# Attention with a threshold, then a mixer: the last key tile stacked, six score buffers, a new order

## The chip, the cores and the metric

The kernel runs on one core of one Trainium2 chip. The metric is the device time in microseconds. The kernel before took 622.38 us (median of 3 runs, 621.68 to 625.62). A core has engines that run on their own: TensorE (PE, with its weight loads listed as PEld) multiplies matrices, VectorE (DVE) and ScalarE (ACT) work on tiles in the two on-chip memories SBUF and PSUM, GpSimd (POOL) works on tiles in SBUF and issues DMAs, SyncE (SP) issues DMAs.

## The reference

The input is q, k and v of 8 batches x 8 heads x 576 positions x 64, a number tau, and the weights of a mixer. The attention keeps only the scores within tau of the row's maximum; a low-rank product over the positions and a two-layer channel mixer follow.

```python
scores = scale * np.matmul(q, k.transpose(0, 1, 3, 2))           # scale = 1/8
thresh = np.max(scores, axis=-1, keepdims=True) - tau
scores = np.where(scores >= thresh, scores, -1000000000.0)
scores = scores - np.max(scores, axis=-1, keepdims=True)
attn = np.exp(scores)
attn = attn / (np.sum(attn, axis=-1, keepdims=True) + 1e-09)
x = np.matmul(attn, v)                  # then heads side by side: (8, 576, 512)
...
h = x.transpose(0, 2, 1) @ U @ V        # U: 576 x 32, V: 32 x 576
u = x + h.transpose(0, 2, 1)
out = u + np.maximum(u @ w_ch1, 0.0) @ w_ch2                     # 512 -> 2048 -> 512
```

## The kernel before

The kernel is written as tasks, each with an engine, a rough cost, what it depends on, and a function that issues its instructions. A scheduler inside the kernel (class `Order`) puts the tasks of each engine into one fixed order when the program is built. Among the tasks that can start, it takes the one with the lowest rank: the moment at which it is ready plus an offset `OFF` by kind of task and by phase (first batch, middle, last batch); the mixer's tasks have a `when`, a number of score steps from which they are due. Where TensorE would stand idle in the scheduler's reckoning, it puts in a filler matmul.

```python
def rank(c):
    s, t = c
    if t.when is not None:
        due = t.when <= steps + (1.0 if t.kind == kind else 0.0)
        return (t.when - 1000.0 if due else t.when + 1000000.0, s)
    return (t.ready + t.off, s)
...
while at[PE] + 0.45 < s and last[n] <= at[PE]:
    self.filler(n)
```

A pair is two heads of one batch; there are 32, four in a batch. Of a pair's 576 queries, four tiles of 128 rows and one of 64 are made; the 64-row tiles of two pairs are joined. So two pairs have nine score steps, 144 in all. A step computes the scores of two heads into PSUM (`scores`, on TensorE), and then, for each head:

```python
# weigh (VectorE): out of PSUM, times -scale, with the row's minimum
nc.vector.tensor_scalar(out=s_sb..., in0=pair_bank[x][:, :, 0:HC], scalar1=-scale, ...,
                        op0=ALU.mult, op1=ALU.min, accum_out=m[:, x:x + 1])
t = add(VEC, 0.69, weigh, [S_, got("w", tiles[0] + x - NS)])     # NS = 4 buffers s_sb
...
# exponential (ScalarE), threshold (ScalarE), then select (VectorE)
nc.scalar.activation(out=e_sb, in_=s_sb, func=ACT.Exp, bias=m[:, x:x + 1], scale=-1.0)
...
nc.vector.scalar_tensor_tensor(out=w_sb[:, 0:S], in0=s_sb, scalar=thr_[:, x:x + 1], in1=e_sb,
                               op0=ALU.is_le, op1=ALU.mult, accum_out=pr.den[:, i, x:x + 1])
```

The weights w_sb (128 queries x 576 keys, padded with zeros to 640) are transposed to keys x queries, by a DMA (`turn_w`) or, for some tiles, on TensorE (`turn_pe`, and `copy_w` on ScalarE). V is split into a high and a low half in bf16:

```python
def high(_):                                      # ScalarE
    nc.scalar.copy(out=pr.vh[:, :, :, 0, :], in_=pr.vraw.rearrange("p j t d -> p t j d"))
def low(_):                                       # GpSimd
    nc.gpsimd.tensor_tensor(out=pr.vh[:, :, :, 1, :],
                            in0=pr.vraw.rearrange("p j t d -> p t j d"),
                            in1=pr.vh[:, :, :, 0, :], op=ALU.subtract)
```

The product multiplies five key tiles (NT = 5, the last with 64 real keys and 64 zeros) with both halves. In the first four pairs (`soft`) the halves are two matmuls of 64 columns into the same place; in the 28 others they stand side by side as one of 128 columns, and their sum is made later (`low_part` on ScalarE, `join` on VectorE, `norm` on GpSimd; in the soft pairs one `make` on VectorE).

```python
for kt in range(NT):
    ...
    first, last_ = kt == 0, kt == NT - 1
    if not soft:
        nc.tensor.matmul(av[:, 2 * a + j, :], w, pr.vh[:, kt, j, :, :], start=first, stop=last_)
        continue
    for h in range(2):
        nc.tensor.matmul(av[:, 2 * a + j, :], w, pr.vh[:, kt, j, h, :],
                         start=first and h == 0, stop=last_ and h == 1)
```

After a pair: `narrow`, `low_rank`, `spread`, `sum_u`, `turn_u` make u and its transpose. After a batch the mixer: 16 groups `up` of four 512-column matmuls, with `relu` on ScalarE, and 4 or 5 tiles of `down` in four quarters of four 512-column matmuls each, with `finish` on VectorE and `send` as a DMA. Every second batch also has `rest`, the up-product of the joined 64-row tiles.

```python
t = add(PE, 0.862, up, uT + weights1 + ..., banks=1, kind="p1", when=due + 35.75 * ft / 16)
...
when = due + 134.5 if i == 4 and b < B - 1 else due + 46.5 + 13.25 * (i + g / 4) / 4
```

Of the kernel before, what the change touches and what calls it, by code (L numbers as in the profile page):

```python
# [8 lines left out]
P = 128  # L9
FP32 = mybir.dt.float32  # L10
BF16 = mybir.dt.bfloat16
# [20 lines left out]
DUE = (30, 48, 66, 87, 163, 120, 127, 156)  # L32
# [32 lines left out]
class Order:  # L65
# [10 lines left out]
    SWITCH = {"quadrants": 0.145, None: 0.095}  # L76
# [4 lines left out]
        "copy_main": (37, 30, -1), "copy_rest": (-1, -8, -1), "copy_tt": (-26, -59, -3),  # L81
        "copy_u": (-22, -16, -2), "copy_u4": (0, 21.25, 0), "copy_w": (39.75, -8, -1),
        "down": (0, 0, 0), "exponential": (21, 43, -29.25), "finish": (-1, 13, -1),
        "first": (-300, 0, 0), "high": (3, -26, -32), "inverse": (-19, 8.75, 8.5),
        "join": (-22, -3.25, 2.5), "load": (16, 20, 2), "low": (0, 0, 0),
        "low_part": (-22, -19.5, -40), "low_rank": (-20, -39, -3), "make": (8.25, -2, -2),
        "narrow": (-24, 15, -5), "narrow_u": (-21, 20.25, -1), "narrow_u4": (1, 9, 1),
        "norm": (-24, -1, -4), "product": (-21, 20, 8), "relu": (-2, -45, -2), "rest": (0, 0, 0),
        "scores": (-26, -69.5, -9), "select": (4.75, 49.25, 0.75), "send": (2, 2, 2),
        "spread": (-23, -7.25, -3), "spread4": (-1, 21, -1), "spread_v": (1, 5, 5),  # L90
        "sum_u": (-25, -11, 0), "sum_u4": (1, -4, 1), "sums": (-22, -1, -1),
        "threshold": (-27, -6, -29.5), "turn4": (-1, -1, -1), "turn_main": (-2, -37.75, -4),
        "turn_pe": (-25, 19.75, -1), "turn_rest": (-3, -38, -5), "turn_u": (-50, -6, -3),
        "turn_w": (-20, 0, 0), "up": (0, 0, 0), "values": (20, 20, 20), "weigh": (-23, -3, -8),
        "weights": (-4, 5, 5),
# [100 lines left out]
def kernel(  # L196
# [33 lines left out]
    idle = wpool.tile([P, 512], BF16, name="idle")  # L230
    nc.vector.memset(idle, 0.0)
# [13 lines left out]
    for t_ in w_ring:  # L245
        nc.vector.memset(t_[:, :, S:640], 0.0)
# [5 lines left out]
    for t_ in vraw_ring:  # L252
        nc.vector.memset(t_[HB:P, :, 4, :], 0.0)
# [16 lines left out]
    NS = 4  # L270
# [20 lines left out]
    def fill(n):  # L291
        nc.tensor.matmul(bank[n], idle[:, 0:P], idle, start=True, stop=True)  # L292
# [24 lines left out]
    def load_tasks(p, pr):  # L317
# [28 lines left out]
        for part, to, of in ((lo, slice(0, 5), slice(0, 5)), (hi, slice(0, 4), slice(5, 9))):  # L346
            def values(_, part=part, to=to, of=of):
                nc.sync.dma_start(pr.vraw[part, :, to, :], vv[:, :, of, :])

            loads["v"].append(add(SP, 0.7, values, freed, dma=0.55))  # L350
# [24 lines left out]
    def prepare_tasks(p):  # L375
# [37 lines left out]
        def low(_):  # L413
            nc.gpsimd.tensor_tensor(out=pr.vh[:, :, :, 1, :],  # L414
                                    in0=pr.vraw.rearrange("p j t d -> p t j d"),
                                    in1=pr.vh[:, :, :, 0, :], op=ALU.subtract)
# [3 lines left out]
        done["vlo", p] = add(POOL, 1.5, low, [t])  # L420
# [6 lines left out]
    def score_tasks(p, i):  # L427
# [51 lines left out]
        for x in range(2):  # L479
# [17 lines left out]
            both = not (p < EARLY and 1 <= i < 4)  # L497

# [14 lines left out]
            if i < 4 and (x == 1 and p < EARLY and i >= 1 or p == NPAIR - 1 and i == 3):  # L513
                t = done["wT", tiles[0]] = add(PE, 0.28, turn_pe, [sel] + free, banks=1,
                                               kind="wT")

                def copy_w(_, x=x, t=t):
                    nc.scalar.copy(
                        out=pr.wT[:, x, :, i * P:(i + 1) * P],
                        in_=bank[t.got[0]][:, 0:320].bitcast(BF16).rearrange(  # L520
                            "p (k r) -> p k r", k=NT))

                t = add(SCA, 0.68, copy_w, [t], frees=[t])
            elif both and not x:
                t = None
                first_sel = sel
            elif both:
                t = done["wT", tiles[0]] = done["wT", tiles[0] - 1] = add(
                    SP, 1.4, turn_w, [first_sel, sel] + free, dma=2.2)
            else:  # L530
                t = done["wT", tiles[0]] = add(SP, 1.28, turn_w, [sel] + free, dma=1.1)
            if t:
                done.setdefault(("wTs", p, i // 2), []).append(t)
                if i == 4:
                    done.setdefault(("wTs", p + 1, 2), []).append(t)
# [11 lines left out]
    def value_tasks(p):  # L547
# [16 lines left out]
        for g, tiles_ in enumerate(((0, 1), (2, 3), (4,))):  # L564
            n = len(tiles_)

            def product(t, tiles_=tiles_):

                av = bank[t.got[0]].rearrange("p (a m) -> p a m", m=D if soft else P)
                for a, i in enumerate(tiles_):  # L570
                    for j in range(2):
                        for kt in range(NT):
# [6 lines left out]
                            first, last_ = kt == 0, kt == NT - 1  # L579
                            if not soft:  # L580
                                nc.tensor.matmul(av[:, 2 * a + j, :], w, pr.vh[:, kt, j, :, :],  # L581
                                                 start=first, stop=last_)
                                continue
                            for h in range(2):
                                nc.tensor.matmul(av[:, 2 * a + j, :], w, pr.vh[:, kt, j, h, :],
                                                 start=first and h == 0, stop=last_ and h == 1)

            av = done["AV", p, g] = add(
                PE, (0.64 if soft else 0.56) * n, product,
# [229 lines left out]
    def weight_loads():  # L819
# [6 lines left out]
        sv = wpool.tile([R, S], FP32, name="sv")  # L826
# [88 lines left out]
```

## Time and profile before

| | busy, us | share of the 618.1 us span |
|---|---|---|
| TensorE matmuls (PE) | 607.7 | 98% |
| VectorE (DVE) | 521.3 | 84% |
| ScalarE (ACT) | 480.1 | 78% |
| GpSimd (POOL) | 290.2 | 47% |

The largest groups: 288 `select` on VectorE, 844 ns each in the mean; 288 `exponential` on ScalarE, 770 ns; 288 `weigh` on VectorE, 752 ns; the scores on TensorE; the mixer's `down` and `up`. Busy time is the union of an engine's instructions, and a matmul's record overlaps the next one's, so the mean of one is longer than the time from one to the next. In the lines shown later, `L461` is `weigh`, `L488` `select`, `L448` the scores, `L581` and `L585` the products with 128 and with 64 columns, `L749` `up`, `L782` `down`, `L414` `low`, `L292` the filler.

### The profile page before, as it was taken

The numbers are of one execution on the slowest core, as the hardware profiler recorded it, in microseconds if no ns is written. First come the engines' busy times: TensorE is split into PE (matmuls) and PEld (weight loads), VectorE is DVE, ScalarE is ACT, GpSimd is POOL, SyncE is SP. The second block draws the span as 40 slices with busy tenths as digits, with TensorE's granted clock in tenths as the row PEclk, the third lists the DMA queues.
The fourth block names the chain that finished last, engine by engine and source line by source line (L and its number), as shares of the span: only waits on it lengthen the run. The fifth ranks groups of instructions, "written<-read, shape, count | busy, mean of one in ns | idle before, by whom it ended". The sixth has DMA issues, their size and how long they took to land.

```text
span 618.1 us, 16905 instructions
## 1 busy us (share of the span) xinstructions
PE 607.7 (98%) x6363; PEld 351.8 (57%) x6363; DVE 521.3 (84%) x1406; ACT 480.1 (78%) x983; POOL 290.2 (47%) x396
## 2 busy tenths in 40 slices
PE   8989999999999999999999999999999999999997
PEld 4555655665666555555565655555466655555553
DVE  5999998799988999799997999899998889797101
ACT  5688899988899678986798877996779956884540
POOL 8976566545455645635465645545365611112000
PEclk9999999999999999999999999999999999999999
DMA  6999999769896897887996997869997876466203
GB/s 153 173 182 186 148 175 156 119 132 152 150 153 129 160 172 147 154 123 158 173 165 139 130 177 151 166 117 160 171 171 128 138 128 123 80 108 104 46 14 72
DMA packets 205105, 86.27 MB, mean 140 GB/s; under 512 B 183136, under 2 KB 195376, under 8 KB 205024
## 3 DMA queue, kind: packets, MB, share of 16 engines
q1 hardware_dynamic: 190016, 62.10, 60.8%
q0 software_dynamic: 14048, 22.76, 19.1%
q8 instruction: 50, 0.82, 0.6%
q10 hardware_dynamic: 960, 0.34, 0.2%
q14 instruction: 31, 0.25, 0.2%
HBM read 36.86 MB, written 9.44 MB: 75 GB/s over the span
## 4 chain that ended last, share of the span: by engine, by line
PE 91%; DVE 4%; DMA 2%; ACT 1%; issue 1%; POOL 0%; SPq 0%; DVEq 0%; ACTq 0%
PE scores L448 25%; PE bank L782 20%; PE bank L749 18%; PE bank L581 13%; PE bank L382 4%; PE bank L765 2%; DVE w_ring L488 2%; DVE s_sb L461 2%; PE bank L642 2%; PE bank L292 1%; PE bank L679 1%; PE bank L657 1%; PE bank L395 1%; DMA vraw_ring<-in_v_dram 1%; PE bank L508 1%
## 5 line engine op out<-in xcount | busy, mean ns | idle before, releaser
L488 DVE SCALAR_TENSOR_TENSOR w_ring<-s_sb,thr,e_sb 128x576 bf16<-128x576 f32 x288 | 236.7, 844 | 8.8 <-ACT e_sb L481 7.1
L481 ACT ACTIVATE e_sb<-s_sb,m 128x576 bf16<-128x576 f32 x288 | 217.9, 770 | 25.8 <-DVE s_sb L461 24.8
L461 DVE TENSOR_SCALAR_CACHE_REDUCE s_sb<-scores 128x576 f32<-128x576 f32 x288 | 207.8, 752 | 33.1 <-PE scores L448 29.4
L448 PE MATMUL scores<-qkT 64*64 64x288 f32 x2304 | 179.8, 415 | 0.8 <-DVE s_sb L461 0.8
L782 PE MATMUL bank<-W2b,R 128*128 128x512 bf16 x576 | 136.9, 379 | 0.0
L629 POOL TENSOR_TENSOR x<-x,rec 128x256 f32<-128x256 f32 (+1 forms) x84 | 60.2, 719 | 142.8 <-DVE x L622 81.6
L749 PE MATMUL bank<-uT,W1b 128*128 128x512 bf16 x512 | 123.6, 379 | 0.0
L448 PEld LDWEIGHTS scores<-qkT 64*64 64x64 f32 x2304 | 77.8, 132 | 75.5 <-issue 15.8
L328 POOL DMA_DIRECT2D qkraw<-in_q_dram x125 | 82.2, 665 | 45.5 <-PE bank L382 37.5
L739 ACT ACTIVATE R<-bank 128x512 bf16<-128x512 f32 x144 | 85.0, 595 | 15.9 <-PE bank L749 11.7
L414 POOL TENSOR_TENSOR vh<-vraw_ring,vh 128x640 bf16<-128x640 f32 x32 | 52.9, 1654 | 90.9 <-ACT vh L410 65.8
L782 PEld LDWEIGHTS <-R 128*128 128x128 bf16 x576 | 53.2, 98 | 56.8 <-issue 5.7
L328 POOL DMA_DIRECT2D qkraw<-in_k_dram x125 | 81.5, 658 | 1.0 <-issue 0.5
L749 PEld LDWEIGHTS <-W1b 128*128 128x128 bf16 x512 | 46.5, 98 | 50.5 <-issue 7.5
L581 PE MATMUL bank<-vh,wT_ring 128*128 128x128 bf16 x1120 | 71.7, 219 | 0.0
L581 PEld LDWEIGHTS <-wT_ring 128*128 128x128 bf16 x1120 | 64.5, 98 | 12.0 <-issue 9.7
L794 DVE TENSOR_TENSOR o<-bank,x 128x512 f32<-128x512 f32 x36 | 24.5, 685 | 38.6 <-PE bank L782 38.2
L474 ACT ACTIVATE thr<-m,tau_t 128x2 f32<-128x2 f32 x144 | 42.0, 292 | 4.2 <-DVE s_sb L461 3.8
L388 ACT COPY qkT<-bank 128x512 f32<-128x512 f32 x64 | 35.7, 584 | 8.7 <-PE bank L382 8.6
L382 PE MATMUL bank<-ident,qkraw 128*128 128x128 f32 x256 | 34.8, 273 | 1.5 <-DMA qkraw<-in_q_dram 1.3
L622 DVE TENSOR_TENSOR x<-bank,x 128x256 f32<-128x256 f32 (+1 forms) x84 | 30.7, 374 | 4.2 <-ACT x L618 3.8
L618 ACT COPY x<-bank 128x256 f32<-128x256 f32 (+1 forms) x84 | 26.6, 330 | 6.9 <-PE bank L581 6.5
(70 smaller groups left out, 497.3 us busy)
## 6 DMA issues: line engine op xcount, KB each, us to landing
out_dram<-o SPq DMA_DIRECT2D x71, 128.0 KB, 2.6
vraw_ring<-in_v_dram SPq DMA_DIRECT2D x32, 160.0 KB, 4.1
qkraw<-in_k_dram POOLq DMA_DIRECT2D x63, 80.0 KB, 4.1
qkraw<-in_q_dram POOLq DMA_DIRECT2D x62, 80.0 KB, 3.9
vraw_ring<-in_v_dram SPq DMA_DIRECT2D x32, 128.0 KB, 4.6
qkraw<-in_q_dram POOLq DMA_DIRECT2D x63, 64.0 KB, 3.8
qkraw<-in_k_dram POOLq DMA_DIRECT2D x62, 64.0 KB, 4.3
W1b<-in_moe_w_ch_dram POOLq DMA_DIRECT2D x8, 256.0 KB, 5.5
```

The costliest lines, as they stand in the source:

```text
L328: queue.dma_start(pr.qkraw[part, to, j, :], src[:, j, of, :])
L382: nc.tensor.transpose(bank[t.got[0]][:, i * P:(i + 1) * P], pr.qkraw[:, t0 + i, :, :], ident)
L414: nc.gpsimd.tensor_tensor(out=pr.vh[:, :, :, 1, :], in0=pr.vraw.rearrange("p j t d -> p t j d"), in1=pr.vh[:, :, :, 0, :], op=ALU.subtract)
L448: nc.tensor.matmul(pair_bank[j][part, c, 0:HC], a.tT[hs, 0, rows], a.tT[hs, 1, cs], start=True, stop=True)
L461: nc.vector.tensor_scalar(out=s_sb.rearrange("p (a c) -> p a c", a=2), in0=pair_bank[x][:, :, 0:HC], scalar1=-scale, scalar2=None, op0=ALU ...
L481: nc.scalar.activation(out=e_sb, in_=s_sb, func=ACT.Exp, bias=m[:, x:x + 1], scale=-1.0)
L488: nc.vector.scalar_tensor_tensor(out=w_sb[:, 0:S], in0=s_sb, scalar=thr_[:, x:x + 1], in1=e_sb, op0=ALU.is_le, op1=ALU.mult, accum_out=pr. ...
L581: nc.tensor.matmul(av[:, 2 * a + j, :], w, pr.vh[:, kt, j, :, :], start=first, stop=last_)
L629: nc.gpsimd.tensor_tensor(out=x, in0=x, in1=over_sum(part), op=ALU.mult)
L739: nc.scalar.activation(out=R2[:, fts, lo:hi], in_=bank[t.got[0]].rearrange("p (f c) -> p f c", c=hi - lo), func=ACT.Relu)
L749: nc.tensor.matmul(bank[t.got[0]], W1b[:, dt, ft * P:(ft + 1) * P], bt.uT[:, dt, :], start=(dt == 0), stop=(dt == 3))
L782: nc.tensor.matmul(ch, R2[:, ft, lo:lo + P], W2b[:, ft, :], start=(ft == 0), stop=(ft == 15))
```

## The change

There are four parts. The key tile with 64 real keys gets the high half of v on partitions 0 to 63 and the low half on 64 to 127, against weights that stand there twice; so hi and lo come out of one matmul of 64 columns. For this, v's last rows are loaded a second time, `low` has two parts, and a copy on GpSimd (`twin`) doubles the weights of the last 64 keys before they are transposed. The score buffers s_sb and e_sb become six. The filler uses the identity matrix in place of a zero tile, and the space comes from there, from sv, and from zeroes that need not be set any more. The ranks (`OFF`, `DUE`, and two of the scheduler's costs) are new; most of `DUE` is above 144, the number of score steps, so most mixer tasks are never due and are taken, in a row by their numbers, where nothing else can start as early.

```diff
-DUE = (30, 48, 66, 87, 163, 120, 127, 156)
+DUE = (218.25, 193.25, 202, 58.75, 370.75, 342.5, 322.25, 741.75)
-    SWITCH = {"quadrants": 0.145, None: 0.095}
+    SWITCH = {"quadrants": 0.17, None: 0.13}
     OFF = {
-        "copy_main": (37, 30, -1), "copy_rest": (-1, -8, -1), "copy_tt": (-26, -59, -3),
+        "copy_main": (-65.55, 4.27, -33.19), "copy_rest": (46.32, -22.93, -32.89), "copy_tt":
+        (55.52, 75.97, 78.39), "copy_u": (-9.24, 32.51, 27.95), "copy_u4": (-33.7, -103.34, 12.57),
 ...                                            (all offsets are new)
-    idle = wpool.tile([P, 512], BF16, name="idle")
-    nc.vector.memset(idle, 0.0)
 ...
-    for t_ in w_ring:
-        nc.vector.memset(t_[:, :, S:640], 0.0)
 ...
-    for t_ in vraw_ring:
-        nc.vector.memset(t_[HB:P, :, 4, :], 0.0)
 ...
-    NS = 4
+    NS = 6
 ...
-        nc.tensor.matmul(bank[n], idle[:, 0:P], idle, start=True, stop=True)
+        nc.tensor.matmul(bank[n].rearrange("p (a c) -> p a c", a=4), identb,
+                         identb.unsqueeze(1).to_broadcast([P, 4, P]), start=True, stop=True)
 ...
-        for part, to, of in ((lo, slice(0, 5), slice(0, 5)), (hi, slice(0, 4), slice(5, 9))):
+        for part, to, of, cost in ((lo, slice(0, 5), slice(0, 5), 0.55), (hi, slice(0, 4), slice(5, 9), 0.5),
+                                   (hi, slice(4, 5), slice(4, 5), 0.15)):
 ...
-            nc.gpsimd.tensor_tensor(out=pr.vh[:, :, :, 1, :],
-                                    in0=pr.vraw.rearrange("p j t d -> p t j d"),
-                                    in1=pr.vh[:, :, :, 0, :], op=ALU.subtract)
+            raw = pr.vraw.rearrange("p j t d -> p t j d")
+            for part, tiles_, h in ((slice(0, P), slice(0, 4), 1), (slice(HB, P), slice(4, 5), 0)):
+                nc.gpsimd.tensor_tensor(out=pr.vh[part, tiles_, :, h, :], in0=raw[part, tiles_],
+                                        in1=pr.vh[part, tiles_, :, 0, :], op=ALU.subtract)
 ...
+            def twin(_, xs=slice(0 if both else x, x + 1)):
+                w_sb = w_ring[n % (NW // 2)]
+                nc.gpsimd.tensor_copy(out=w_sb[:, xs, S:640], in_=w_sb[:, xs, 512:S])
+
+            twin_ = add(POOL, 0.3, twin, [sel] + ([first_sel] if both else []))
 ...                                            (turn_w and turn_pe wait for twin_, not for sel)
-                            first, last_ = kt == 0, kt == NT - 1
+                            if kt == NT - 1:
+                                nc.tensor.matmul(av[:, 2 * a + j, 0:D], w, pr.vh[:, kt, j, 0, :],
+                                                 start=False, stop=True)
+                                continue
                             if not soft:
                                 nc.tensor.matmul(av[:, 2 * a + j, :], w, pr.vh[:, kt, j, :, :],
-                                                 start=first, stop=last_)
+                                                 start=kt == 0, stop=False)
                                 continue
                             for h in range(2):
                                 nc.tensor.matmul(av[:, 2 * a + j, :], w, pr.vh[:, kt, j, h, :],
-                                                 start=first and h == 0, stop=last_ and h == 1)
+                                                 start=kt + h == 0, stop=False)
 ...
-        sv = wpool.tile([R, S], FP32, name="sv")
+        sv = x_ring[2].rearrange("p a m -> p (a m)")[0:R, 0:S]
```

## The prediction

> **What bounds the kernel now.** I read the page's table of busy time first, then the busy time by stretch, then the chain of waits, then the timeline of VectorE and GpSimd, because the first answer (TensorE is full) is true of one part of the run only.
>
> ```profile
> PE 607.7 (98%) x6363; PEld 351.8 (57%) x6363; DVE 521.3 (84%) x1406; ACT 480.1 (78%) x983; POOL 290.2 (47%) x396
> ...
> PE 91%; DVE 4%; DMA 2%; ACT 1%; issue 1%; POOL 0%; SPq 0%; DVEq 0%; ACTq 0%
> ```
>
> TensorE is busy 98% of the span and is 91% of the chain that ended last. The busy time by stretch (columns: stretch, its length, then busy time and count of PE, PEld, DVE, ACT, POOL, granted clock, DMA share, GB/s) splits this in three:
>
> ```profile
> 15.00:80.00 65.00, 61.95 (x906) 38.41 (x899) 64.72 (x180) 53.31 (x106) 47.03 (x67) 1.00 1.16 176
> 80.00:560.00 480.00, 480.00 (x5030) 278.88 (x5029) 435.23 (x1172) 398.98 (x827) 227.17 (x303) 1.00 0.83 144
> 560.00:597.00 37.00, 36.78 (x281) 21.06 (x280) 10.41 (x23) 20.16 (x38) 3.72 (x6) 1.00 0.30 54
> ```
>
> Up to 80 us VectorE is the bound: 64.72 of 65 us. TensorE looks busy there too, but part of it is filler (62 matmuls on a zero tile, 17.9 us in all) and part is score matmuls drawn out by a wait. From 80 to 560 us TensorE has no gap, while VectorE still has 91%. After 560 us only the mixer's matmuls are left. The chain of waits (start, length, piece; the last column counts instructions) shows the same change and also gives prices, because a piece on the chain is time really passed, while the mean duration of a matmul is not:
>
> ```profile
> 41.56 1.35 DVE s_sb L461 x4
> ...
> 45.74 1.48 DVE w_ring L488 x4
> ...
> 55.83 1.33 PE bank L585 x40
> ...
> 61.53 1.27 PE bank L585 x40
> ...
> 303.80 2.23 PE bank L581 x40
> ```
>
> A pair of `weigh` with its accumulator reads takes 1.35 us, a pair of `select` 1.48 us. In the product of the weights with V, a matmul of 128 columns takes 2.23/40 = 56 ns; one of 64 columns (first batch) takes 1.27 to 1.33 us / 40 = 32 to 33 ns.
>
> **What the Trainium skill says.** (1) "TensorE: Matmul & The Clock Gate", section "Back-to-back issue gap": in a stream of weight load and matmul the spacing is set by both; about 81 ns at 128 columns. The trace gives 56 ns, so the measurement decides; but that half the columns don't halve the spacing (33, not 28 ns) fits the sentence. (2) "SBUF — State Buffer", section "Who interferes with whom": a VectorE instruction with two SBUF inputs and a GpSimd instruction that reads SBUF take one shared read port; the one that comes second waits for the whole of the first. `select` reads s_sb and e_sb, so it is of this kind; `weigh` reads PSUM and is not. The trace agrees. The timeline (start, length, engine, line, operation) at 289 us has a `low` on GpSimd from 289.49 to 291.20, and the `select` that begins inside it takes 1.61 us instead of 0.81:
>
> ```profile
> 289.13 0.81 DVE L488 SCALAR_TENSOR_TENSOR w_ring<-s_sb,thr,e_sb 128x576 bf16<-128x576 f32 x1
> ...
> 289.49 1.71 POOL L414 TENSOR_TENSOR vh<-vraw_ring,vh 128x640 bf16<-128x640 f32 x1 [5.01 <-ACT vh L410]
> ...
> 290.21 1.61 DVE L488 SCALAR_TENSOR_TENSOR w_ring<-s_sb,thr,e_sb 128x576 bf16<-128x576 f32 x1
> ```
>
> (3) "Perfetto Trace Analysis", section "Identifying the Most-Contended Engine": TensorE's matmul busy share is a poor measure of headroom. That is why I price by the chain and not by 219 ns, the mean of one 128-column product in this trace.
>
> **The change part by part.**
>
> *Stacking, on TensorE.* The fifth key tile has only 64 real keys. Now partitions 0 to 63 carry v's high half, 64 to 127 the low half, and one product of 64 columns replaces hi and lo. In the 28 later pairs: 28 x 5 query tiles x 2 heads = 280 products go from 56 to 33 ns: 280 x 0.023 = 6.4 us. In the first 4 pairs: 4 x 5 x 2 = 40 products vanish: 40 x 0.033 = 1.3 us. The 1.3 us falls before 80 us, where TensorE waits anyway, and is hidden. The 6.4 us falls in the stretch without gaps and counts in full: -6.4 us.
>
> *Fillers.* The instruction order of the changed kernel has 78, not 62. The place matters more: 57 of the 62 stand before the 23rd score step, which began at 80.2 us, then 2 in that step and 3 in the 31st. In the changed order all 78 stand before the 23rd. So the gapless stretch loses 5 x 0.216 = 1.1 us (0.216 us: 1.73 us / 8 from the chain for matmuls of 512 columns); the 16 more lie in front of it, where VectorE sets the pace. -1.1 us.
>
> *The twin, on GpSimd.* The weights of the last 64 keys are copied beside themselves before the transpose: 168 new copies (120 of 2 x 64, 48 of 64 elements). The trace has none like it. The fastest `low` does 640 elements with two inputs in 1393 ns, 2.2 ns each; the slowest kind of copy there, a strided cast, 256 in 1170 ns, 4.6 ns each. So I estimate 0.3 to 0.5 us for 128 elements, some 50 to 60 us of GpSimd in all: from 290 to about 345 us, 56% of the span, no bound. But it reads SBUF and comes right behind a `select`, so it takes the shared port at the busiest place. A twin that waits for a `select` gets the port as that ends; if the next instruction is a `weigh`, it costs nothing. I take one in five to hold up a `select` by 0.3 us: 168 x 0.06 = 10 us of VectorE. Of these, 37 twins belong to the first 22 score steps: 37 x 0.06 = 2.2 us on the path that sets the pace there. That the transposes start some 0.4 us later lies off that path. +2.2 us.
>
> *`low`* splits in two (512 elements, then 128 on 64 partitions), one more issue on GpSimd 32 times, and one more DMA of 32 KB per pair. Both lie beside other work: 0. *The memsets* taken out (idle, w_ring, vraw: 0.27 + 0.45 + 0.33 us) stand on VectorE before 10 us, where the first load (landed at 6.8 us) decides: 0.
>
> *Six score buffers.* `weigh` of a step needs s_sb released by the `select` four tiles back; with six, one more step can be in flight. In the first 80 us VectorE has work of 67.2 us up to its 22nd pair of `weigh` (counted from its order with 0.675 us a `weigh`, 0.765 a `select`, 0.34 a `make`, 0.61 a `sum_u`) between 10.1 and 80.3 us, so at most 3 us of idle, half-hidden stalls and port waits can be won; the new order also puts 0.8 us less before that point. I book -1.5 us for both.
>
> *New ranks.* In the gapless stretch a new order alone wins nothing: there is no gap to close. It can lose. From the 23rd to the 144th score step TensorE took 476.8 us (3.94 us a step); counting the groups in both orders at the chain's prices (1.13 us a score step, 0.2 for its two changes of array mode, 0.865 a group of four 512-column matmuls, 56 or 33 ns a product; scaled by 0.986 so that the old order gives the measured time) the new one takes 8.7 us less (3.87 a step), because 3 us more of the mixer is left for the tail. VectorE is busy 435.2/121 = 3.60 us a step; with its share of the twins 3.68. That is 95%, and over the last 16 steps, where the new order gives TensorE only 3.70 us a step, nearly all. I book +1.5 us for gaps there.
>
> Sum: -6.4 - 1.1 + 2.2 - 1.5 + 1.5 = -5.3 us; 622.4 - 5.3 = 617.1 us.
>
> **The rivals.** (a) *VectorE becomes the bound.* For it: 91% already, and the port. Against it: 435 of 480 us leaves 45 us of slack. If each twin cost a `select` 0.3 us (50 us), the gain is gone: 622 to 635 us. (b) *GpSimd's queue delays the transposes.* It issues the q and k loads too (0.66 us each), in order; a twin behind a waiting load keeps w_ring and the product late. For it: 47.0 of 65 us busy before 80 us, and 37 twins of 0.3 to 0.5 us make that about 60. Against it: 24 of GpSimd's waits are for ACT on vh, 65.8 us in all, so most of its idle time is spare. It would show as 3 to 8 us in the first 100 us: 620 to 625. (c) *The new order starts the gapless stretch earlier.* If six buffers and the ranks bring the 23rd step to 76 us, the time is 612 to 613. (d) *Lumps in the new order*: between steps 84 and 85 ten `up` groups stand in a row, 8.65 us in which VectorE gets no new scores. TensorE stays busy, so VectorE only has to catch up later; at 3.6 us a step against 3.9 it does. Worth 0 to 3 us.
>
> **Range and chances.** The certain term is TensorE's 7.5 us; the others are each 1 to 3 us with unsure sign, and (a), (b) lean to the slow side, (c) to the fast. 610 to 624 us should hold it 8 times in 10. Faster by 2% means below 609.9: it takes (c) in full and no loss, 7%. Slower by 2% is above 634.8: it takes (a) almost in full, 5%. Within 2%: 88%.
>
> **What would show each step right or wrong.** Stacking: the 64-column products at about 33 ns spacing, and PE work after the 23rd step smaller by 6 to 8 us. Fillers: none after about 80 us. Twin: its group in the table at 0.3 to 0.5 us x168, and `select` no longer than 0.90 us in the mean (844 ns now); rival (a) would put it above 0.95 and show idle TensorE with VectorE as releaser. The 23rd step later than 82 us speaks for (b), earlier than 78 for (c). The prediction is wrong if TensorE has gaps of more than 5 us in all between 80 and 590 us, or if the last score step is later than 557 us.

## The result, and the profile after

The changed kernel takes 615.87 us (median of 4 runs, 614.68 to 618.81), against 622.12 us (621.68 to 625.62) for the kernel before beside it: the ratio is 0.9897, with an interval of 0.9861 to 0.9933. A later comparison gave 614.78 us and 0.9889 [0.9871, 0.9907]. The prediction was 617.1 us, 610 to 624.

The page's table of busy time and the shares of the chain of waits, of the kernel after:

```profile
PE 600.8 (98%) x6339; PEld 346.1 (56%) x6339; DVE 521.0 (85%) x1399; ACT 478.3 (78%) x983; POOL 361.2 (59%) x596
...
PE 73%; DVE 1%; issue 1%; ACT 0%; DVEq 0%
```

TensorE has lost 6.9 us of busy time and still fills 98% of a shorter span; GpSimd has gained 71 us and bounds nothing. The chain is not comparable in its shares: after, it can be followed back only to 150 us, and 73% is all of TensorE's part of that stretch; the rest of the span is simply not in it. The busy time by stretch, kernel after (stretch, length, busy time and count of PE, PEld, DVE, ACT, POOL, granted clock, DMA share, GB/s):

```profile
15.00:80.00 65.00, 62.44 (x888) 38.79 (x891) 63.55 (x182) 53.30 (x108) 48.14 (x85) 1.00 0.95 154
80.00:560.00 480.00, 478.35 (x5084) 276.67 (x5079) 443.43 (x1186) 401.94 (x837) 299.20 (x486) 1.00 0.87 151
560.00:597.00 37.00, 37.00 (x249) 19.79 (x247) 5.86 (x9) 15.91 (x29) 0.84 (x2) 1.00 0.18 40
```

The split in three has stayed: VectorE nearly full up to 80 us, TensorE nearly full from then on, with 1.65 us of gaps where there were none. GpSimd has 72 us more from 80 to 560 us and only 1 us more from 15 to 80, though 32 twins (13.8 us) lie there: the groups of that stretch list 28 loads of q and k where there were 47. The loads come later now, which will matter below. The 23rd score step begins at 79.7 us (80.2 before), and the 144th at 549.3 (557.0 before).

The timeline of TensorE, kernel after (start, length, engine, line, operation; `L592` is the product with 128 columns, `L588` the stacked one with 64):

```profile
332.59 0.39 PE L592 MATMUL bank<-vh,wT 128*128 128x128 bf16 x4
332.81 0.19 PE L588 MATMUL bank<-vh,wT 128*128 128x64 bf16 x1
332.84 0.39 PE L592 MATMUL bank<-vh,wT 128*128 128x128 bf16 x4
333.07 0.19 PE L588 MATMUL bank<-vh,wT 128*128 128x64 bf16 x1
333.10 0.59 PE L760 MATMUL bank<-uT,W1b 128*128 128x512 bf16 x2
```

The lengths overlap, so read the starts: the narrow matmul is followed by the next one 0.03 us later, and a group of five takes 0.25 to 0.26 us. I added up the times from one start to the next, from the 23rd score step to the last matmul:

```
                                         before            after
products with V, us (number)             80.3 (1400)       63.4 (1120 wide) + 10.8 (280 narrow) = 74.2
fillers                                   1.2 (5)           0
everything else                         451.4             454.0
23rd step to last matmul                532.9             528.2
```

The narrow product is followed by the next matmul after 28 ns at the median and 38.7 in the mean: 25 of the 280 stand before a score step, and there the next start comes after some 122 ns (one of them 0.67 us; after a wide product in the kernel before it was 149 ns). The wide product is at 56 ns as before. The products give 6.1 us (6.4 in the second profile), the fillers 1.2; everything else has grown by 2.6 us. TensorE's gaps grow by 1.4 us in all (0.2 to 1.6), the scores with what follows them by 0.9; the two overlap. The groups on GpSimd and the `select`, kernel after (operation, shape, count, busy time and mean ns, idle time before):

```profile
L489 DVE SCALAR_TENSOR_TENSOR w_ring<-s_sb,thr,e_sb 128x576 bf16<-128x576 f32 x288 | 240.0, 861 | 4.5 <-ACT e_sb L482 2.6
...
L507 POOL COPY w_ring<-w_ring 128x128 bf16<-128x128 bf16 (+1 forms) x168 | 71.1, 430 | 121.2 <-DVE w_ring L489 87.2
...
L416 POOL TENSOR_TENSOR vh<-vraw_ring,vh 128x512 bf16<-128x512 f32 x64 | 58.5, 914 | 11.7 <-ACT vh L409 8.8
```

`select` went from 844 to 861 ns, far from the 950 of rival (a). `low` takes 58.5 us in 64 pieces where it took 52.9 in 32.

### The profile page after: what moved, and what is told of

The parts are those of the page before. It is cut to its first block, busy times and chain, and to the rows that moved or that the text cites. A ratio compares the mean times of both kernels' runs of the same rounds, so it can differ in the third digit from the quotient of the medians.

```text
span 612.9 us, 17317 instructions
## 1 busy us (share of the span) xinstructions
PE 600.8 (98%) x6339; PEld 346.1 (56%) x6339; DVE 521.0 (85%) x1399; ACT 478.3 (78%) x983; POOL 361.2 (59%) x596
## 4 chain that ended last, share of the span: by engine, by line
PE 73%; DVE 1%; issue 1%; ACT 0%; DVEq 0%
PE scores L449 19%; PE bank L793 18%; PE bank L760 16%; PE bank L592 9%; PE bank L381 3%; PE bank L776 2%; PE bank L653 1%; PE bank L588 1%; PE bank L668 1%; PE bank L690 1%; PE bank L394 1%; DVE w_ring L489 1%; DVE s_sb L462 0%; PE bank L705 0%; PE bank L727 0%
## 5 line engine op out<-in xcount | busy, mean ns | idle before, releaser
L489 DVE SCALAR_TENSOR_TENSOR w_ring<-s_sb,thr,e_sb 128x576 bf16<-128x576 f32 x288 | 240.0, 861 | 4.5 <-ACT e_sb L482 2.6
L507 POOL COPY w_ring<-w_ring 128x128 bf16<-128x128 bf16 (+1 forms) x168 | 71.1, 430 | 121.2 <-DVE w_ring L489 87.2
L750 ACT ACTIVATE R<-bank 128x512 bf16<-128x512 f32 x144 | 83.0, 592 | 19.2 <-PE bank L760 13.6
L326 POOL DMA_DIRECT2D qkraw<-in_q_dram x125 | 82.1, 663 | 13.8 <-PE bank L381 7.5
L640 POOL TENSOR_TENSOR x<-x,rec 128x256 f32<-128x256 f32 (+1 forms) x84 | 57.4, 685 | 52.4 <-DVE x L633 41.3
L416 POOL TENSOR_TENSOR vh<-vraw_ring,vh 128x512 bf16<-128x512 f32 x64 | 58.5, 914 | 11.7 <-ACT vh L409 8.8
L592 PE MATMUL bank<-vh,wT_ring 128*128 128x128 bf16 x896 | 64.3, 219 | 0.0
L592 PEld LDWEIGHTS <-wT_ring 128*128 128x128 bf16 x896 | 55.5, 98 | 7.6 <-issue 4.4
L588 PE MATMUL bank<-vh,wT_ring 128*128 128x64 bf16 x256 | 49.3, 193 | 0.3 <-POOL vh L416 0.3
```

What stands on the lines that cost most here:

```text
L326: queue.dma_start(pr.qkraw[part, to, j, :], src[:, j, of, :])
L416: nc.gpsimd.tensor_tensor(out=pr.vh[part, tiles_, :, h, :], in0=raw[part, tiles_], in1=pr.vh[part, tiles_, :, 0, :], op=ALU.subtract)
L507: nc.gpsimd.tensor_copy(out=w_sb[:, xs, S:640], in_=w_sb[:, xs, 512:S])
L640: nc.gpsimd.tensor_tensor(out=x, in0=x, in1=over_sum(part), op=ALU.mult)
L750: nc.scalar.activation(out=R2[:, fts, lo:hi], in_=bank[t.got[0]].rearrange("p (f c) -> p f c", c=hi - lo), func=ACT.Relu)
```

## The experiments

My theory: the gain is the narrow products in the stretch without gaps and the fillers there; the new order and the buffers add next to nothing by themselves, and the twin costs about 2 us. Rivals: the new order or the six buffers brought the gain, and the narrow products are hidden; or the twin costs far more and something else pays for it. All medians, with the ratio to the kernel before and its interval, the start of the 23rd score step, and the time from there to the last matmul (the last two from one profiled run, which lies up to 3.2 us from the median). The runs came from several chips, on which the kernel before took 621.3 to 622.7 us; each ratio is to the kernel before on the same chip, so kernels of different chips are compared by their ratios.

| kernel | us | ratio | 23rd step | from there |
|---|---|---|---|---|
| before | 622.1 | 1 | 80.2 | 532.9 |
| after, again | 614.78 | 0.9889 [0.9871, 0.9907] | 80.4 | 528.2 |
| late_wide | 621.46 | 1.0005 [0.9986, 1.0024] | 80.5 | 534.2 |
| early_twice | 616.28 | 0.9902 [0.9876, 0.9929] | 81.0 | 528.3 |
| no_twin | 630.37 | 1.0136 [1.0116, 1.0156] | 94.7 | 527.5 |
| two_twins | 623.91 | 1.0027 [1.0001, 1.0052] | 82.4 | 531.5 |
| tiny_twin | 616.02 | 0.9893 [0.9869, 0.9918] | 82.2 | 527.3 |
| w1_later | 622.91 | 0.9996 [0.9976, 1.0017] | 87.7 | 530.0 |
| new_order_only | 632.95 | 1.0177 [1.0125, 1.0228] | 84.7 | 542.2 |
| placeholder | 625.62 | 1.0062 [1.0044, 1.0080] | 86.3 | 534.9 |
| stack_only | 628.58 | 1.0092 [1.0067, 1.0117] | 86.6 | 534.7 |
| six_only | 630.38 | 1.0133 [1.0102, 1.0164] | 82.6 | 541.1 |
| four_buffers | 627.20 | 1.0077 [1.0052, 1.0101] | 86.2 | 534.1 |

The last two columns are the key to the table: what happens before the 23rd step and what happens after it add up.

### The changed kernel again

> The changed kernel once more, on the same chip as the three others of this set, as their base. Both theories expect 614 to 618 us and a gapless TensorE from the 23rd to the last score step, within 2 us.

614.78 us (614.48 to 615.37, 5 runs): the yardstick for the experiments that edit the kernel after.

### Where the gain is: the narrow products made wide again

The 280 products of the last key tile outside the first four pairs get 128 columns again. To have 128 columns without touching anything else they multiply with the two halves of key tile 3, so the output is not the attention's.

```diff
                             if kt == NT - 1:
+                                if not soft:
+                                    nc.tensor.matmul(av[:, 2 * a + j, :], w, pr.vh[:, 3, j, :, :],
+                                                     start=False, stop=True)
+                                    continue
                                 nc.tensor.matmul(av[:, 2 * a + j, 0:D], w, pr.vh[:, kt, j, 0, :], ...)
```

> The 280 products of the last key tile in the 28 later pairs are 128 columns wide again (they take the fourth tile's values of v, so the output is not the reference's); everything else, the order of every engine, twin and buffers too, is as in the changed kernel. Theory (the gain is TensorE's saved columns in a stretch where TensorE has no gap): 280 x 17 to 23 ns come back, +5 to +6.5 us against the changed kernel, and the last score step comes at 553 to 556 us, not 549. Rival (the gain comes from the new order and the six buffers, and the narrow products only make gaps elsewhere): within 1.5 us of the changed kernel, with TensorE's gaps smaller instead.

Measured: 621.46 us (620.74 to 626.74), 6.7 us more than the kernel after and the same as the kernel before. The timeline of TensorE in late_wide (`L596` and `L589` are the first four and the last key tile):

```profile
332.90 0.39 PE L596 MATMUL bank<-vh,wT_ring 128*128 128x128 bf16 x4
333.13 0.22 PE L589 MATMUL bank<-vh,wT_ring 128*128 128x128 bf16 x1
333.18 0.39 PE L596 MATMUL bank<-vh,wT_ring 128*128 128x128 bf16 x4
333.41 0.22 PE L589 MATMUL bank<-vh,wT_ring 128*128 128x128 bf16 x1
```

A group of five now takes 0.28 us. The start of the score steps shows the difference grow evenly, which is what a price per product looks like, and not what a single stall looks like:

```
score step        26      56      86     116     144
after, again    92.1   207.2   327.3   442.3   550.0
late_wide       91.8   208.0   329.8   446.4   555.8
```

So the narrow products are the gain. It also follows that all the rest together (order, buffers, twin, fillers) comes out at about nothing: 621.46 us against 621.74 for the kernel before on the same chip, with an interval on both sides of 1; the fillers' 1.2 us are in that, paid back by gaps and slower groups.

### The products saved in the first four pairs

The 40 products that vanish there are issued again (the last tile is multiplied twice, so its part is counted double in those pairs).

```diff
                             if kt == NT - 1:
+                                if soft:
+                                    nc.tensor.matmul(av[:, 2 * a + j, 0:D], w, pr.vh[:, kt, j, 0, :],
+                                                     start=False, stop=False)
```

> In the first four pairs the product of the last key tile is done twice (40 matmuls of 64 columns more, the number that stacking took out there; the output counts that tile twice in the first batch and is not the reference's). All orders stay. Theory (before the 23rd step TensorE waits for VectorE, so these 1.3 us are hidden): within 0.7 us of the changed kernel. Rival (TensorE bounds that part too): 1.3 us or more slower.

Measured: 616.28 us (616.06 to 618.95), 1.5 us more than after_again, or 0.8 by the ratios, whose intervals overlap. The 23rd step comes 0.6 us later, and the time from there is the same. That the 1.3 us are hidden is compatible with this and not shown by it; about half may come through.

### The twin left out

The task keeps its place in the scheduler's order but issues nothing; the padding is zeroed as before. The low half of the last 64 keys is left out of the result.

```diff
+    for t_ in w_ring:
+        nc.vector.memset(t_[:, :, S:640], 0.0)
             def twin(_, xs=slice(0 if both else x, x + 1)):
                 w_sb = w_ring[n % (NW // 2)]
-                nc.gpsimd.tensor_copy(out=w_sb[:, xs, S:640], in_=w_sb[:, xs, 512:S])
+                return
```

> The 168 copies on GpSimd that double the last 64 keys' weights are left out (the second copy stays at zero, so the low half of the last 64 values is missing in the output); the order of every engine is otherwise that of the changed kernel. Theory (a twin now and then holds up a select on the shared read port, some 0.06 us each, and only the share before the 23rd step is on the path): 1.5 to 4 us faster than the changed kernel, the 23rd step at 76 to 78.5 us in place of 79.7, the mean of select back from 861 to about 845 ns. Rival A (twins are hidden altogether): within 1 us. Rival B (twins take most of VectorE's slack): 6 us faster or more.

Measured: 630.37 us (628.96 to 631.06): 15.6 us slower, where I expected less work to be faster. After the 23rd step it is as fast as the kernel after (527.5 against 528.2 us); all is lost before it. The mean of `select` is 874 ns, not the 845 I expected, so the twins are not what makes it longer. The chain of waits of no_twin has two long pieces there (start, length, piece):

```profile
34.25 11.01 DMA wT_ring<-w_ring
...
72.62 14.83 DMA wT_ring<-w_ring
```

A DMA transpose of the weights takes 11 and 15 us to land. The busy time by stretch of no_twin shows what that does (columns as above):

```profile
70.00:80.00 10.00, 7.46 (x98) 4.51 (x90) 7.69 (x22) 5.39 (x12) 5.25 (x7) 0.87 1.35 130
80.00:90.00 10.00, 5.51 (x77) 4.64 (x69) 3.92 (x12) 3.21 (x7) 1.91 (x5) 0.67 1.20 105
```

From 80 to 90 us VectorE is busy for 3.92 of 10 us, TensorE for 5.51, and its clock falls to 0.67; the DMA engines have a higher share than in the 10 us before these lines (1.10) and move less (130 and 105 GB/s, 185 before). What has changed on the way there is when GpSimd issues its loads. Its timeline in no_twin:

```profile
15.70 2.58 POOL L328 DMA_DIRECT2D qkraw<-in_q_dram  x4 [0.25 <-PE bank L396]
18.26 2.58 POOL L328 DMA_DIRECT2D qkraw<-in_k_dram  x4
...
28.37 1.13 POOL L855 DMA_DIRECT2D W1b<-in_moe_w_ch_dram  x2
...
31.81 2.69 POOL L328 DMA_DIRECT2D qkraw<-in_q_dram  x4
```

and in the kernel after (again):

```profile
20.03 0.63 POOL L326 DMA_DIRECT2D qkraw<-in_q_dram  x1
...
21.89 0.98 POOL L507 COPY w_ring<-w_ring 128x64 bf16<-128x64 bf16 x2 [0.62 <-DVE w_ring L489]
22.87 1.30 POOL L326 DMA_DIRECT2D qkraw<-in_k_dram  x2
...
35.86 1.13 POOL L853 DMA_DIRECT2D W1b<-in_moe_w_ch_dram  x2 [0.24 <-issue]
...
42.17 2.69 POOL L326 DMA_DIRECT2D qkraw<-in_q_dram  x4
```

GpSimd takes its tasks in order. With the twin, a load that stands behind it waits for VectorE's `select` (the 0.62 us in the bracket are such a wait); the loads come out mostly in ones and twos between the twins. Without it they come out in fours and run ahead: the same two loads of w_ch1 at 28 instead of 36 us, the same four of q at 32 instead of 42. The Trainium skill, "DMA: Bandwidth & Descriptors", section "Issuing engines are not separate DMA queues", says that DMAs started by ScalarE, SyncE or GpSimd end up on the same 16 DMA engines and interleave there. That is what the transposes, issued by SyncE, run into. It holds up both sides: the four loads of w_ch2 issued from 66 to 81 us land after 11.2 us at the median and 13.9 at most, where those issued up to 100 us in the kernel after (again) took 5.6 and 7.1. The view of the transposes into wT_ring (the tiles of 128 queries) ends with the time from issue to landing; from 52 to 100 us, no_twin:

```profile
DMA to landing us min/median/max: 2.6/5.1/16.0
```

and the kernel after (again):

```profile
DMA to landing us min/median/max: 3.2/4.9/7.0
```

The median is the same; it is a few transposes that are hit.

### The twin doubled, and the twin of one column

Two questions: what one more twin costs, and whether it is the copy that matters or its place in GpSimd's order.

```diff
                 nc.gpsimd.tensor_copy(out=w_sb[:, xs, S:640], in_=w_sb[:, xs, 512:S])
+                nc.gpsimd.tensor_copy(out=w_sb[:, xs, S:640], in_=w_sb[:, xs, 512:S])    # two_twins
```

> Each of the 168 twin copies is done twice over (same result, same order). GpSimd gets 168 x 0.42 = 71 us more, 432 us of some 613. Theory (small cost by the shared port, mostly before the 23rd step): 1.5 to 5 us slower than the changed kernel, mean of select 870 to 890 ns. Rival A (hidden): within 1 us. Rival B (VectorE or GpSimd near its limit): 8 us slower or more, and TensorE shows gaps of over 5 us between 80 and 560 us, released by VectorE or by the transposes.

Measured: 623.91 us (620.04 to 627.44), 9.1 us more. GpSimd has 414.8 us of work, `select` 878 ns. The profiled run (620.70 us) is one of the quickest and accounts for 5.3 us: 2.0 up to the 23rd step, 3.3 after it, where the recorded gaps grow from 1.6 to 3.9 us. One more instruction for each twin is not free. The median is in the range of rival B, but its gaps of over 5 us don't show in the profiled run; what the slower runs lose stays open.

```diff
+    for t_ in w_ring:
+        nc.vector.memset(t_[:, :, S:640], 0.0)
-                nc.gpsimd.tensor_copy(out=w_sb[:, xs, S:640], in_=w_sb[:, xs, 512:S])
+                nc.gpsimd.tensor_copy(out=w_sb[:, xs, 639:640], in_=w_sb[:, xs, 575:S])   # tiny_twin
```

One column of 64 is copied, so nearly all of the low half of the last 64 keys is left out; the instruction and its waits stay.

> Every twin copies one column in place of 64 (the other 63 stay at zero, so most of the low half of the last 64 values is missing in the output). It still stands at its place in GpSimd's queue and waits for its select. Without the twins the kernel took 630.4 us, and there GpSimd issued the q, k and weight loads up to 11 us earlier, and one transpose took 14.8 us to land. Theory (a twin's wait holds back the loads that stand behind it, and that keeps the transposes quick; its own copy costs a little): 611 to 615 us, the 23rd step at 77 to 80 us, no transpose of the first 100 us over 8 us. Rival (the copies themselves, not their place in the queue, are what was missing): 622 us or more, with slow transposes as in the kernel without twins.

Measured: 616.02 us (615.14 to 617.44), by its ratio like the kernel after. The instruction with its place in the order is worth about 15 us against no_twin, by the ratios, and the other 63 columns cost nothing that can be seen; `select` is at 861 ns here too. The copy is not shortened by much, though: one column takes 0.19 us undisturbed, 64 take 0.24 or 0.29. And not all went as the theory said: the 23rd step comes at 82.2 us, and the slowest transpose of the first 100 us takes 8.9 us.

### The loads moved, the twin kept

If late transposes come from loads that run into them, moving loads with everything else kept should move the late transposes. Three of the eight loads of w_ch1 (each 128 x 1024 of W1b) are issued at 57 and 61 us, together with two that stand there anyway, and not from 36 to 42 us.

```diff
         def w1(_, t, h):
-            cs = slice(h * (F // 2), (h + 1) * (F // 2))
-            nc.gpsimd.dma_start(W1b[:, t, cs], moe_w_ch1[t * P:(t + 1) * P, cs])
+            for t, h in {(1, 0): (), (2, 0): (), (3, 0): (), (1, 1): ((1, 0), (1, 1)),
+                         (2, 1): ((2, 0), (2, 1), (3, 0))}.get((t, h), ((t, h),)):
+                cs = slice(h * (F // 2), (h + 1) * (F // 2))
+                nc.gpsimd.dma_start(W1b[:, t, cs], moe_w_ch1[t * P:(t + 1) * P, cs])
```

> The changed kernel, with three of the eight loads of w_ch1 (256 KB each) moved back in GpSimd's queue: the second to fourth, issued at 36 to 42 us, are now issued beside the sixth and seventh, at 57 to 62 us. Nothing else moves. Three transposes issued from 39 us on held SyncE for 10.3 us in the changed kernel and 16.2 in the run with the placeholder, right behind these loads. Theory (these loads share the 16 DMA engines with the transposes and delay them): transposes between 36 and 52 us land in under 5 us at most, not up to 7.3, and the 23rd step comes at 77 to 80.5 us; 611 to 616 us, if the loads do not collide with the next transposes at 60 us. Rival (the late transposes have another cause): the same 7 us or more at 36 to 52 us. What speaks against using it: a new collision at 57 to 70 us, 617 us or more.

Measured: 622.91 us (621.80 to 624.43), 6.7 us more than the kernel after by the ratios; the 23rd step starts at 87.7 instead of 80.4 us. GpSimd's timeline in w1_later:

```profile
57.08 1.14 POOL L855 DMA_DIRECT2D W1b<-in_moe_w_ch_dram  x2
...
61.36 1.63 POOL L855 DMA_DIRECT2D W1b<-in_moe_w_ch_dram  x3
```

The landing times of the transposes into wT_ring in w1_later, first from 36 to 52 us, then from 52 to 100:

```profile
DMA to landing us min/median/max: 2.9/3.9/4.6
...
DMA to landing us min/median/max: 3.5/4.8/12.6
```

and in the kernel after (again) from 36 to 52 us:

```profile
DMA to landing us min/median/max: 4.1/4.9/7.3
```

Where the loads left, the slowest transpose is down from 7.3 to 4.6 us; where they went, it is up from 7.0 to 12.6. The collision went with the loads. This is the one experiment that moves only the suspected cause, and it shows it for these transposes. That the same collision costs no_twin its 14 us before the 23rd step is read from its chain, which holds the two late transposes, and not from an experiment of its own.

### The parts alone

new_order_only is the kernel after without the stacking and without the twin (the transposes wait for `select`); new ranks and six buffers stay. The scheduler makes another order of it. placeholder keeps the kernel after's order, with a copy of one column into a scratch tile in the twin's place. Both compute the whole reference.

```diff
-            twin_ = add(POOL, 0.3, twin, [sel] + ([first_sel] if both else []))      # new_order_only
 ...
-                nc.gpsimd.tensor_copy(out=w_sb[:, xs, S:640], in_=w_sb[:, xs, 512:S])
+                nc.gpsimd.tensor_copy(out=scratch[:, xs, :], in_=w_sb[:, xs, 575:S])   # placeholder
 ...         (products, low and the zeroes as before, in both; the second load of v's last rows stays in placeholder)
```

> New ranks, six score buffers and the identity as filler, but v and the product as in the kernel before: hi and lo as 128 columns over all five key tiles, no twin. Theory (all of the gain is the narrow product and some fillers): 619 to 624 us. Rival A (the new order and the six buffers bring part of it): 618 us or less. Rival B (without twins in GpSimd's queue the loads run ahead and the transposes are late, as in the kernel without twins): 626 us or more, with transposes of over 8 us in the first 100 us.

> The changed kernel's order, six buffers and loads, but the product and low as in the kernel before (128 columns for all five key tiles; the doubled values of v meet zero weights). In the twin's place GpSimd copies one column to a scratch tile after each select, which nothing needs. Theory (what the twins do for the early part is to hold back the loads behind them in GpSimd's queue; the new order itself gains nothing in time): 620 to 623 us, as the kernel before, with the 23rd step at 80 to 82 us. Rival (the new order, unstacked, is slow in itself): 628 us or more, as in the run with the new order alone (633.0).

Measured: 632.95 us (630.96 to 645.78), as rival B said, and 625.62 us (622.33 to 628.45), between theory and rival. The chain of new_order_only has late transposes again:

```profile
37.51 10.22 DMA wT_ring<-w_ring
57.12 8.64 DMA wT_ring<-w_ring
448.15 8.52 DMA wT_ring<-w_ring
482.99 7.18 DMA wT_ring<-w_ring
```

two of them far behind the 23rd step, where the time grows too (542.2 us, with 4.4 us of gaps and 8 fillers). placeholder takes 7.3 us less after the 23rd step (534.9 us, as in late_wide, which has wide products too). The early part stays long in the profiled run: its chain has one transpose of 11.37 us at 35.36 us, and the 23rd step comes at 86.3 us. That run took 628.13 us, 2.5 more than the median, so the early part of most runs may be shorter. So an instruction in the twin's place holds the loads back, but doesn't guarantee that they miss the transposes: a program with slightly different timings runs into them all the same.

stack_only is the kernel before with the stacking and the twin (its rank -20), the old ranks and four buffers. six_only is the kernel before with six buffers, and the filler and sv changed to make room. four_buffers is the kernel after with four.

```diff
-    NS = 4
+    NS = 6                      # six_only; the other way round in four_buffers
 ...
-        "turn_w": (-20, 0, 0), "up": (0, 0, 0), ...
+        "turn_w": (-20, 0, 0), "twin": (-20, -20, -20), "up": (0, 0, 0), ...      # stack_only
```

> The kernel before with the stacked last tile alone: four score buffers, old ranks, twin with a rank offset of -20 in all phases. The order of the instructions has 17 fillers behind the 23rd step (0.216 us each, 3.7 us), the kernel before has 5. Theory (6 us less on TensorE, 2.6 us more fillers, twins cost some 2 us before the 23rd step): 617 to 621 us. Rival (the twins need a new order, or else the early part gets longer): 623 us or more and the 23rd step at 84 us or later.

> The kernel before with six score buffers in place of four, old ranks (the identity as filler and sv in a tile that is free then, for the space). The scheduler's order has 70 fillers, 13 behind the 23rd step (5 before). Theory (VectorE has at most 3 us to win before the 23rd step, and TensorE is full after it): 620 to 625 us. Rival (four buffers hold VectorE back): 618 us or less.

> The changed kernel with four score buffers and the same new ranks. The scheduler makes another order of it: 110 fillers, 18 of them behind the 23rd step and 12 of these after the last score step. Theory (the ranks were made for six buffers; fillers of 3.9 us and a later 23rd step): 620 to 630 us. Rival (the buffers don't matter): 616 to 619 us.

Measured: 628.58 us (627.48 to 629.52), 630.38 us (629.71 to 631.53) and 627.20 us (625.60 to 628.59), all slower than the kernel before. four_buffers lies in the range of its theory; six_only (expected at 620 to 625) and stack_only (617 to 621) do not, and stack_only does what its rival said. It has narrow products and still takes longer after the 23rd step than the kernel before (534.7 us): the scheduler, which reckons with its own costs, puts 17 fillers there (4.0 us), and the gaps are 3.4 us. And the 23rd step comes 6 us later. Two early stretches of stack_only, and the second of them in the kernel after (again):

```profile
20.00:40.00 20.00, 18.19 (x261) 11.82 (x258) 18.93 (x58) 14.88 (x29) 15.09 (x29) 0.93 1.12 154
40.00:60.00 20.00, 17.10 (x237) 10.78 (x238) 15.62 (x41) 15.20 (x31) 17.13 (x27) 0.90 0.93 159
...
40.00:60.00 20.00, 18.45 (x275) 11.20 (x267) 19.44 (x54) 17.75 (x37) 15.15 (x26) 1.00 1.12 172
```

VectorE is 15.62 of 20 us busy from 40 to 60 us, with 19.44 in the kernel after. Yet the slowest transpose into wT_ring of the first 100 us lands in 7.6 us (7.3 there), so the early loss is not the collision above; the waits are spread over many releasers, and what sets them off stays open. After the 23rd step the chain of stack_only does have two late transposes, 6.37 us at 159.81 and 8.51 us at 184.27. four_buffers loses in the same two ways, by 18 fillers (4.5 us) and a later 23rd step. six_only loses 2.4 us before the 23rd step and 8.2 after it: 1.7 by more fillers (13), 2.6 by gaps, and the rest spread over several groups, which I did not follow further.

No kernel of the study beats the kernel after.

## Why the prediction was right

The time was 617.1 against 615.9 and 614.8 us measured, and the main reason holds. By its steps:

- *Stacking, -6.4 us*: right in mechanism, and in size partly by luck. The products' starts give -6.1 to -6.4 us, taking the width back costs 6.7. But the price of 33 ns was misread: the piece of the chain, divided by 40, runs to the end of the last matmul's record, which is 0.19 us long. In the same trace the 40 products at 55.83 us start 29 ns apart (1.133 us from the first start to the last), so half the columns do nearly halve the spacing, against what I concluded in point (1) of the prediction. At 28 ns I would have booked 280 x 28 = 7.8 us. Changes to a score step and a few waits behind the products, which I had not priced, take 1.5 to 1.7 us of that back. The two errors nearly cancel.
- *The 1.3 us of the first pairs hidden*: not contradicted.
- *Fillers, -1.1 us*: right, 1.2, and none after the 23rd step.
- *Twin, +2.2 us*: its duration was about right (0.43 us in the mean; 71 us of GpSimd, put at 50 to 60), its price was mis-sized, and the way to it did not hold. I charged it for holding up one `select` in five by 0.3 us, 10 us of VectorE. In the trace 23 `select`s begin inside a twin and together take 0.1 us longer than the median. It is the other way round: a twin alone takes 0.24 us (64 elements) or 0.29 (128), and the 52 that begin inside a `select` take 0.76 in the mean. The Trainium skill, "SBUF — State Buffer", section "Who interferes with whom", calls the shared ports an exclusive lock and says that the order of issue decides who blocks. The trace agrees for the twin behind a `select`; a `select` behind a twin shows next to nothing of it (spans on GpSimd are rough). The longer `select` goes in part with `low`: 30 `select`s begin inside one, with 6.7 us above the median in all, against 10 with 3.5 us before. That `low` now has two pieces is not what makes `select` longer: in placeholder it has one, in the same order, and `select` is at 859 ns all the same. With two pieces and the old ranks (stack_only) it is at 851. So it goes with the new order.
- *Six buffers and new order up to the 23rd step, -1.5 us*: with the twin I had booked +0.7 there; it was -0.5 (79.7 against 80.2 us) in one profile and +0.2 in the other. How this sum near nothing divides stays open. The count above puts the twin's part near nothing, while in two_twins a second copy for each twin takes 2.0 us up to there. Six buffers alone, or four under the new ranks, are slower, but the scheduler makes another order of each.
- *Gaps, +1.5 us*: right, 1.4. From the 23rd step to the 144th TensorE takes 469.6 us, 3.88 a step (put at 3.87). VectorE's 3.68 a step counted all 168 twins where 131 fall there; with these it is 3.66. *`low`, 0*: no cost shows by itself, though the `select`s beside it are longer.
- *Rival (a)*, VectorE as the bound: not there. *Rival (b)*, GpSimd's queue holding back the transposes: not in this kernel, and its sign was wrong in kind. I thought of a twin stuck behind a load. What counts is a load stuck behind a twin, and that helps. Its size (3 to 8 us up to 100 us) is about what other orders lose, by late transposes or for reasons left open; only no_twin, with 14, is outside. *Rival (c)*, 76 us: no. *Rival (d)*: the last score step starts 7.7 us earlier, so no lump was worth more than the gaps above.

What I did not see was how narrow the ground is. I treated the order as nearly free to vary, with ±1.5 us; with the new ranks kept, placeholder and new_order_only take 4 and 11 us more than late_wide, which like them has wide products, and four_buffers 12 us more than the kernel after. The range was wide enough because the kernel after happens to be a good member of that family, and nothing in the profile of the kernel before would have told me.

## What to carry to other kernels

Price a matmul by the time from one start to the next, in the stretch where TensorE has no gap: the recorded length of a product (219 ns) is four times that price (56 ns), and even a piece of the chain divided by its count gave 33 ns where the starts give 29. Then ask which matmul stands behind it, because a change of work costs too (122 ns before a score step, not 28). In a kernel with a fixed order on every engine, removing an instruction is a change of the order: look at what stood behind it in its queue, loads above all, and where these will now land. And a part that gains in one order can lose in another, so a part's worth is measured by taking it out of the finished kernel with the order kept, and not by adding it to the old one.

## What the runs showed of the hardware

- DMA transposes issued by SyncE, in the median 5 us from issue to landing, took 10 to 16 us when loads issued by GpSimd ran into them, and the loads landed late too; moving three loads moved this with them.
- GpSimd's order works as a brake on its loads: the same program with the twins' 168 instructions left out is 15.6 us slower, and with them shrunk to one column it is not.
- A copy of 64 or 128 bf16 elements a partition on GpSimd takes 0.24 or 0.29 us; begun inside a `select` of VectorE it takes 0.76 in the mean, while a `select` begun inside a copy is hardly longer.
- Matmuls of 64 columns, each with its own weights, follow one another in 28 or 29 ns (median), those of 128 in 56.
